# An attention and gated-MLP block on one core: reordered by a scheduler that runs at build time, part of the exponentials moved to VectorE, and full-width matmuls split into four column tiles

## The chip, the core and the metric

The kernel runs on one core of a Trainium2 chip. The metric is the time of one execution on the device in microseconds (us); lower is better. TensorE multiplies matrices, ScalarE takes exponentials, VectorE does elementwise work and copies, GpSimd does some of that too, and SyncE issues DMAs. The profile records one execution with the start, the end and the wait of every instruction, and the share of its clock that TensorE was granted (1.0 is full, 0.5 is half). "The trace" is that record, "the page" is its printed summary.

A run is called slow when it is more than 1.5% above the fastest run of the same kernel. The ratios use the fast runs; the medians are of all runs.

## The reference

One sequence of 2048 rows of 640 columns passes through a 32-head attention block (20 columns per head) and a gated MLP (1728 columns). Both have a layer norm ahead and a residual around them. All is bf16.

```python
def _A_ref(x, wqkv, wo):
    B, S, D = x.shape; H = 32; Dh = D // H          # 1, 2048, 640; Dh = 20
    q, k, v = ...(x @ wqkv) split into heads...
    scores = jnp.einsum("bhqd,bhkd->bhqk", q, k) * (Dh ** -0.5)
    p = softmax(scores, axis=-1)
    o = jnp.einsum("bhqk,bhkd->bhqd", p, v)
    return o.transpose(0, 2, 1, 3).reshape(B, S, D) @ wo
def _B_ref(x, w_gate, w_up, w_down):
    h = (x @ w_gate) * (x @ w_up)
    return h @ w_down
h  = x + _A_ref(_layernorm(x), wqkv, wo)
h2 = h + _B_ref(_layernorm(h), w_gate, w_up, w_down)
return h2
```

The scores are 32 x 2048 x 2048 exponentials. Spread over 128 partitions they make 2048 banks of 512 columns (a bank here is a PSUM tile of 128 x 512 in f32). That is the work around which both kernels are built.

## The kernel before

Attention runs in four passes of 512 queries. In a pass, each of eight groups of four heads goes through sixteen tiles of 128 keys. One step makes four score banks, takes their exponentials as two instructions of 1024 columns, and multiplies them with V ("PV") into one accumulator. All other matmuls are background: a Python generator emits some of it after each half step, a budget of 440 ns at a time. During the first pass the background is the K, Q and V projections; during every later pass it is the output projection and the MLP of the pass ahead (the one just finished).

```python
sA   = ctx.enter_context(tc.tile_pool(name="sA", bufs=3, space=PSUM))    # scores, 3 x 2 banks
accp = ctx.enter_context(tc.tile_pool(name="accp", bufs=1, space=PSUM))  # PV accumulator
mp   = ctx.enter_context(tc.tile_pool(name="mp", bufs=1, space=PSUM))    # all background: ONE bank
# ... cut ...
for c in range(KC):                       # gate, of second_stage(); up is alike
    nc.tensor.matmul(pg[0:M, :], lhsT=wg[:, c, o:o + M], rhs=ln2T[:, c, :],
                     start=(c == 0), stop=(c == KC - 1))
    yield 220
gs = p2s.tile([P, QW], F32, name="gs", tag="gs")
nc.vector.tensor_copy(gs[0:M, :], pg[0:M, :])
# ... cut ...
def emit_S(n):                            # two score banks: row tiles of the array, 32 rows each
    for i, j in enumerate(hs_):
        nc.tensor.matmul(sp[:, i, :], lhsT=kT[g][32*j:32*j+32, kt*P:(kt+1)*P],
                         rhs=qT[qc][32*j:32*j+32, g, :], start=True, stop=True)
def emit_exp(n):
    nc.scalar.activation(E[:], sp[:], ACT.Exp, scale=LN2_ / UNIT)         # 1024 columns
def emit_PV(s):                           # four column tiles, 32 columns each
    for j in range(HP):
        nc.tensor.matmul(acc[32*j:32*j+32, :], lhsT=Vx[kt][:, h*VS:h*VS+32],
                         rhs=E_of.pop((s, j)), start=(kt == 0), stop=(kt == NT - 1))
# ... cut ...
for n in range(N + LAG):
    if n + LEAD < N:
        emit_S(n + LEAD)
    if n < N:
        emit_exp(n)
    for s in pv_at.get(n, ()):
        emit_PV(s)
        # at the end of a pass: finish all background, then queue second_stage(qc)
    advance(440)
while bg:
    advance(1 << 30)                      # the last pass's output projection and MLP: the tail
```

The softmax here doesn't subtract the row's maximum and nothing guards it: scores larger than these inputs give would overflow.

Of the kernel before, what the change touches and what calls it, by code (L numbers as in the profile page):

```python
# [10 lines left out]
F32 = mybir.dt.float32  # L11
ACT = mybir.ActivationFunctionType
# [3 lines left out]
P = 128  # L16
# [9 lines left out]
NQ = S // QW  # L26
# [5 lines left out]
VW = H * VS + 32 - VS  # L32
# [3 lines left out]
EPS_B = 1.0013580322265625e-05  # L36


@with_exitstack
def kernel(  # L40
# [17 lines left out]
    dram = ctx.enter_context(tc.tile_pool(name="dram", bufs=4, space=bass.MemoryType.DRAM))  # L58


    const = ctx.enter_context(tc.tile_pool(name="const", bufs=1))
    keep = ctx.enter_context(tc.tile_pool(name="keep", bufs=1))
    xpool = ctx.enter_context(tc.tile_pool(name="xpool", bufs=1))
    epool = ctx.enter_context(tc.tile_pool(name="epool", bufs=6))
    npool = ctx.enter_context(tc.tile_pool(name="npool", bufs=2))
    tiny = ctx.enter_context(tc.tile_pool(name="tiny", bufs=2))
    lnp = ctx.enter_context(tc.tile_pool(name="lnp", bufs=1))

    sA = ctx.enter_context(tc.tile_pool(name="sA", bufs=3, space=PSUM))
    accp = ctx.enter_context(tc.tile_pool(name="accp", bufs=1, space=PSUM))  # L70
    mp = ctx.enter_context(tc.tile_pool(name="mp", bufs=1, space=PSUM))


    xt = [xpool.tile([P, TPC, D], BF16, name=f"x{c}", tag=f"x{c}") for c in range(NQ)]
    p1 = tc.alloc_tile_pool(name="p1", bufs=1, side="right")
    Wr = [p1.tile([P, 3 * D], BF16, name=f"Wr{c}", tag=f"Wr{c}") for c in range(KC)]
    for tt in range(TPC):
        nc.sync.dma_start(xt[0][:, tt, :], x2d[tt * P:(tt + 1) * P, :])
    for c in range(KC):
        eng = nc.scalar if c % 2 == 0 else nc.sync  # L80
        eng.dma_start(Wr[c][:, 0:2 * D], A_wqkv[c * P:(c + 1) * P, 0:2 * D])
    for c in range(KC):
        nc.sync.dma_start(Wr[c][:, 2 * D:3 * D], A_wqkv[c * P:(c + 1) * P, 2 * D:3 * D])
    for ch in range(1, NQ):
        nc.sync.dma_start(
            xt[ch][:], x2d[ch * QW:(ch + 1) * QW, :].rearrange("(t p) d -> p t d", p=P))

    ident = const.tile([P, P], BF16, name="ident")
    make_identity(nc, ident[:])
    half = const.tile([P, TPC], F32, name="half")  # L90
    nc.gpsimd.memset(half[:], 0.5)
    warm = const.tile([P, 1], F32, name="warm")
    nc.scalar.activation(warm[:], half[:, 0:1], ACT.Exp)

    kT = [keep.tile([P, S], BF16, name=f"kT{g}", tag=f"kT{g}") for g in range(G)]
    qT = [(p1 if ch == 0 else keep).tile([P, G, QW], BF16, name=f"qT{ch}", tag=f"qT{ch}")
          for ch in range(NQ)]
    Vx = [keep.tile([P, VW], BF16, name=f"Vx{t}", tag=f"Vx{t}") for t in range(NT)]
    OnT = [keep.tile([P, QW], BF16, name=f"On{g}", tag=f"On{g}") for g in range(G)]

    Wp = [[p1.tile([P, G * P], BF16, name=f"Wp{b}{c}", tag=f"Wp{b}{c}") for c in range(KC)]
          for b in range(2)]
    lnT = p1.tile([P, KC, S], BF16, name="lnT")
    for b in (1, 0):
        for c in range(KC):
            wv = Wp[b][c][:].rearrange("p (h e) -> p h e", e=32)
            nc.gpsimd.memset(wv[:, :, DH:32], 0.0)
    for t in range(NT):
        nc.gpsimd.memset(
            Vx[t][:, 0:H * VS].rearrange("p (h e) -> p h e", e=VS)[:, :, DH:VS], 1.0)  # L110
        nc.gpsimd.memset(Vx[t][:, H * VS:VW], 0.0)


    def ln_stats(srcs):
        mv = tiny.tile([P, TPC, 2], F32, name="mv", tag="mv")
        for i, s in enumerate(srcs):
            st = tiny.tile([P, 2, 6], F32, name="st", tag="st")
            for c in range(2):
                nc.vector.bn_stats(st[:, c, :], s[:, c * HD:(c + 1) * HD])  # L119
            nc.vector.bn_aggr(mv[:, i, :], st[:])  # L120
        vb = tiny.tile([P, TPC], BF16, name="vb", tag="vb")
        nc.vector.tensor_copy(vb[:], mv[:, :, 1])
        ve = tiny.tile([P, TPC], BF16, name="ve", tag="ve")
        nc.vector.tensor_scalar_add(ve[:], vb[:], EPS_B)
        den = tiny.tile([P, TPC], BF16, name="den", tag="den")
        nc.gpsimd.tensor_tensor(den[:], ve[:], half[:], ALU.pow)
        rstd = tiny.tile([P, TPC], F32, name="rstd", tag="rstd")
        nc.vector.reciprocal(rstd[:], den[:])
        return mv, rstd

    def ln_apply(s, i, mv, rstd):
        ln = lnp.tile([P, D], BF16, name="ln", tag=f"ln{i}")
        nc.vector.tensor_scalar(ln[:], s, mv[:, i, 0:1], rstd[:, i:i + 1],  # L133
                                ALU.subtract, ALU.mult)
        return ln

    def transposed(lns, dst, copy):

        for c0 in range(0, KC, 2):
            n = min(2, KC - c0)  # L140
            pt = mp.tile([P, 2, QW], BF16, name="pt", tag="m")
            for c in range(n):
                for i, ln in enumerate(lns):
                    nc.tensor.transpose(pt[:, c, i * P:(i + 1) * P],  # L144
                                        ln[:, (c0 + c) * P:(c0 + c + 1) * P], ident[:])
                    yield 70
            copy(dst(c0, n), pt[:, 0:n, :])


    def proj_k(g, ch, b):  # L150
        sl = slice(ch * QW, (ch + 1) * QW)
        ps = mp.tile([P, QW], F32, name="pk", tag="m")
        for c in range(KC):
            nc.tensor.matmul(ps[:], lhsT=Wp[b][c][:, g * P:(g + 1) * P], rhs=lnT[:, c, sl],  # L154
                             start=(c == 0), stop=(c == KC - 1))
            yield 220
        if b == 1:
            nc.vector.tensor_copy(kT[g][:, sl], ps[:])
        else:
            nc.vector.tensor_scalar_mul(qT[ch][:, g, :], ps[:], KAPPA)  # L160

    def proj_v(t, hf):
        ps = mp.tile([P, HD], F32, name="pv", tag="m")
        for c in range(KC):
            nc.tensor.matmul(ps[:], lhsT=lnT[:, c, t * P:(t + 1) * P],  # L165
                             rhs=Wr[c][:, 2 * D + hf * HD:2 * D + (hf + 1) * HD],
                             start=(c == 0), stop=(c == KC - 1))
            yield 140
        nh = H // 2
        nc.vector.tensor_copy(  # L170
            Vx[t][:, hf * nh * VS:(hf + 1) * nh * VS].rearrange("p (h e) -> p h e", e=VS)[:, :, 0:DH],
            ps[:].rearrange("p (h e) -> p h e", e=DH))

    done = set()

    def run(gen):
        for _ in gen:
            pass

    def lnT_dst(ch):  # L180
        return lambda c0, n: lnT[:, c0:c0 + n, ch * QW:(ch + 1) * QW]

    def ln1(ch):
        mv, rstd = ln_stats([xt[ch][:, i, :] for i in range(TPC)])
        return [ln_apply(xt[ch][:, i, :], i, mv, rstd) for i in range(TPC)]


    lns = ln1(0)
    for b in (1, 0):
        for c in range(KC):  # L190
            nc.scalar.copy(
                Wp[b][c][:].rearrange("p (h e) -> p h e", e=32)[:, :, 0:DH],
                Wr[c][:, b * D:(b + 1) * D].rearrange("p (h e) -> p h e", e=DH))
    run(transposed(lns, lnT_dst(0), nc.vector.tensor_copy))
    run(proj_k(0, 0, 1))
    run(proj_k(0, 0, 0))
    done |= {("K", 0, 0), ("Q", 0, 0)}
    ln_next = ln1(1)

    def first_stage():  # L200
        nonlocal ln_next
        for t in range(TPC):
            yield from proj_v(t, 0)
            done.add(("V", t, 0))
        for ch in range(1, NQ):
            yield from transposed(ln_next, lnT_dst(ch), nc.vector.tensor_copy)
            yield from proj_k(0, ch, 1)
            done.add(("K", 0, ch))
            if ch + 1 < NQ:
                ln_next = ln1(ch + 1)  # L210
            for t in range(ch * TPC, (ch + 1) * TPC):
                yield from proj_v(t, 0)
                done.add(("V", t, 0))
        vq = deque(range(NT))
        for g in range(1, G):
            yield from proj_k(g, 0, 0)
            done.add(("Q", g, 0))
            for ch in range(NQ):
                yield from proj_k(g, ch, 1)
                done.add(("K", g, ch))  # L220
# [79 lines left out]
    for n, (_, s, hs_) in enumerate(units):  # L300
        last_unit[s] = n
# [142 lines left out]
```

## Time and profile before

The time was 1791.87 us (median of 3 runs, 1779.78 to 1798.72).

| reading | value |
|---|---|
| TensorE, ScalarE, VectorE busy | 81%, 56%, 15% |
| exponentials | 1024 of 1024 columns, 994.5 us busy |
| first exponential; last one ends; tail after it | 23.2 us; 1627.6 us; 158 us |
| granted clock | mean 0.60 as listed, 0.56 with the head corrected (see below) |

These are lines of the page of the kernel before: busy time, the busy share and the clock in tenths over 40 slices of the span, the chain of waits that ended last, and the group of the exponentials (busy us, mean ns, then idle time ahead and what ended it).

```profile
span 1785.0 us, 15333 instructions
...
PE 1453.2 (81%) x6000; PEld 333.1 (19%) x6000; DVE 261.4 (15%) x512; ACT 1002.4 (56%) x1036; POOL 59.5 (3%) x90
...
PE   4678789889947898989958989999778898996677
...
ACT  3235445445954454699944545999544458994000
...
PEclk9999655555556555865565555755555558555557
...
PE 55%; ACT 18%; DVE 11%; issue 8%; DMA 5%; SPq 2%; POOL 1%; POOLq 0%; DVEq 0%; ACTq 0%
...
L335 ACT ACTIVATE E<-sp 128x1024 bf16<-128x1024 f32 x1024 | 994.5, 1298 | 619.1 <-PE sp L325 618.4
```

TensorE is busy and heads the chain, while ScalarE idles 619 us in wait of scores. The clock row says that TensorE ran at half clock nearly all the time. Its first slices are false. The trace's first clock record begins at 154.5 us, and the page prints 1.0 where it has none; but near 101 us the timeline shows back-to-back matmuls of 320 columns starting every 240 to 270 ns (columns of the fence: start, duration, engine, line, operation):

```profile
101.43 0.45 PE L165 MATMUL pv<-Wr_97,lnT 128*128 128x320 bf16 x1
101.67 0.47 PE L165 MATMUL pv<-Wr_98,lnT 128*128 128x320 bf16 x1
101.94 0.47 PE L165 MATMUL pv<-Wr_99,lnT 128*128 128x320 bf16 x1
```

At recorded full clock (around 750 us) matmuls of the same size start every 136 ns. So the head ran at half clock too, and in the whole span only 204 us were at full clock.

Every listed mean clock has this fault. In the traces of the experiments it is worth 0.03 or less, but in a run without a trace the head is unknown: 8 of the 29 runs of the old kernel beside the experiments list 0.70 to 0.73, and they are no faster (1766.92 to 1803.19 us). A false head that reached to the second rise of the clock in this trace, at 550.4 us, would list 0.70 (an estimate from this trace). So the listed mean of an untraced run shows little.

What a half-clock stage looks like is seen in TensorE's timeline of the kernel before, during gate and up:

```profile
640.76 0.61 PE L325 MATMUL sp<-qT_136,kT_128 32*128 32x512 bf16 x2
641.30 0.62 PE L349 MATMUL acc<-E,Vx_147 128*32 128x512 bf16 x4
641.85 1.03 PE L264 MATMUL pg<-ln2T,wg 128*128 128x512 bf16 x2
642.82 0.61 PE L325 MATMUL sp<-qT_136,kT_128 32*128 32x512 bf16 x2
```

A 512-column matmul streams for 427 ns at this clock: behind a matmul of its own shape, 96 of 122 back-to-back starts of full-width matmuls in this trace are 426 or 427 ns apart. Each change of tile shape (scores in row tiles, PV in column tiles, background at full width; "mode" in some places below) adds about 110 ns (medians of 107 to 113 ns between scores, PV and the start of background; about 100 ns at full clock): from 640.76 to 641.30 the score pair takes 540 ns and not 427. The texts below call this gap a drain; the trace shows its length and not what TensorE does in it. The old order made 1837 such changes, counted in the order of starts in the trace.

Next, windows of the kernel before (columns: window, length, busy us with count for TensorE, weight loads, VectorE, ScalarE and GpSimd, then granted clock, DMA share, GB/s): gate and up, pure attention, and the tail.

```profile
640.00:660.00 20.00, 18.20 (x61) 2.97 (x60) 2.76 (x4) 10.26 (x11) 0.00 (x0) 0.50 0.03 8
...
840.00:860.00 20.00, 18.50 (x92) 3.46 (x88) 0.00 (x0) 20.00 (x23) 1.26 (x1) 0.50 0.04 14
...
1627.00:1785.00 158.00, 102.78 (x340) 41.13 (x337) 36.51 (x68) 0.61 (x1) 2.27 (x2) 0.59 0.13 34
```

With background in the mix TensorE is full and ScalarE half used. When a pass has run out of background, ScalarE is full: an exponential of 1024 columns every 0.917 us (38 in a row from 840.8 us), of which 1024 take about 939 us.

### The profile page before, as it was taken

What the parts mean: (1) busy time and instruction counts of PE and PEld (TensorE: products, weight loads), DVE (VectorE), ACT (ScalarE), POOL (GpSimd) and SP (SyncE); (2) the same over time, 40 slices, a digit from 0 to 9 for tenths busy, and PEclk for the clock granted to TensorE, in tenths of its full rate; (3) what the DMA queues carried; (4) which work ended last, traced back from release to release, by engine and by line L of the source; (5) the groups of instructions that cost most, each with busy time, mean ns of one, the idle gap of its engine ahead of it and who ended that gap; (6) DMA issues with size and microseconds to landing.
All of it is one profiled execution on the core that took longest, in us unless ns stands there. A gap on an engine that the chain in (4) does not pass through costs nothing.

```text
span 1785.0 us, 15333 instructions
## 1 busy us (share of the span) xinstructions
PE 1453.2 (81%) x6000; PEld 333.1 (19%) x6000; DVE 261.4 (15%) x512; ACT 1002.4 (56%) x1036; POOL 59.5 (3%) x90
## 2 busy tenths in 40 slices
PE   4678789889947898989958989999778898996677
PEld 1222111111102111221121112211211122111223
DVE  4411111111002111100021111000021111000321
ACT  3235445445954454699944545999544458994000
POOL 1000000000010000000000000000000000000000
PEclk9999655555556555865565555755555558555557
DMA  3000000000013101000011010000102100001010
GB/s 114 0 1 6 7 7 0 7 7 0 9 31 78 36 15 32 18 11 13 7 36 29 22 32 10 18 7 13 36 1 51 33 2 20 13 7 42 23 48 15
DMA packets 60128, 38.33 MB, mean 21 GB/s; under 512 B 17496, under 2 KB 55320, under 8 KB 60056
## 3 DMA queue, kind: packets, MB, share of 16 engines
q1 hardware_dynamic: 59624, 36.37, 7.9%
q8 instruction: 47, 0.77, 0.2%
q10 hardware_dynamic: 432, 0.98, 0.2%
q14 instruction: 25, 0.20, 0.0%
HBM read 34.19 MB, written 2.88 MB: 21 GB/s over the span
## 4 chain that ended last, share of the span: by engine, by line
PE 55%; ACT 18%; DVE 11%; issue 8%; DMA 5%; SPq 2%; POOL 1%; POOLq 0%; DVEq 0%; ACTq 0%
ACT E L335 18%; PE sp L325 14%; PE pk L154 8%; PE pg L264 7%; PE acc L349 7%; PE pu L271 7%; PE py L284 5%; PE pv L165 2%; PE po L243 2%; DVE hh L275 2%; DMA rs<-accS 2%; SPq L359 2%; DVE gs L268 1%; DMA rb<-rd 1%; DVE st L119 1%
## 5 line engine op out<-in xcount | busy, mean ns | idle before, releaser
L335 ACT ACTIVATE E<-sp 128x1024 bf16<-128x1024 f32 x1024 | 994.5, 1298 | 619.1 <-PE sp L325 618.4
L264 PE MATMUL pg<-ln2T,wg 128*128 128x512 bf16 (+1 forms) x280 | 143.7, 617 | 59.1 <-DVE hh L275 45.5
L271 PE MATMUL pu<-ln2T,wu 128*128 128x512 bf16 (+1 forms) x280 | 144.1, 618 | 21.4 <-DVE gs L268 21.4
L284 PE MATMUL py<-Wd,hh 128*128 128x320 bf16 x448 | 98.6, 347 | 16.8 <-DVE ot L287 13.7
L356 DVE COPY accS<-acc 128x512 f32<-128x512 f32 x32 | 22.1, 692 | 405.2 <-PE acc L349 405.2
L268 DVE COPY gs<-pg 128x512 f32<-128x512 f32 (+1 forms) x56 | 38.5, 688 | 207.9 <-PE pg L264 207.9
L275 DVE TENSOR_TENSOR hh<-gs,pu 128x512 bf16<-128x512 f32 (+1 forms) x56 | 38.3, 684 | 203.5 <-PE pu L271 203.5
L144 PE MATMUL pt<-ident,ln 128*128 128x128 bf16 x160 | 25.6, 303 | 52.1 <-DVE ln L133 39.7
L284 PEld LDWEIGHTS <-hh 128*128 128x128 bf16 x448 | 41.9, 106 | 67.0 <-issue 49.9
L271 PEld LDWEIGHTS <-wu 128*128 128x128 bf16 (+1 forms) x280 | 27.4, 117 | 97.8 <-issue 97.8
L154 PE MATMUL pk<-lnT,Wp_168 128*128 128x512 bf16 x32 | 18.2, 570 | 29.1 <-DVE qT_135 L160 6.4
L264 PEld LDWEIGHTS <-wg 128*128 128x128 bf16 (+1 forms) x280 | 26.1, 120 | 83.2 <-issue 70.2
L243 PE MATMUL po<-wo,On_162 128*128 128x320 bf16 x32 | 11.6, 362 | 35.3 <-POOL On_162 L368 35.3
L243 PE MATMUL po<-wo,On_155 128*128 128x320 bf16 x32 | 11.7, 365 | 31.0 <-DMA wo<-in_A_wo_dram 26.9
L325 PEld LDWEIGHTS <-kT_128 32*128 32x128 bf16 x256 | 13.0, 98 | 125.4 <-issue 125.4
L165 PE MATMUL pv<-Wr_96,lnT 128*128 128x320 bf16 x32 | 12.6, 393 | 28.9 <-DVE Vx_147 L170 5.1
L325 PEld LDWEIGHTS <-kT_129 32*128 32x128 bf16 x256 | 13.1, 99 | 116.0 <-issue 115.8
L287 DVE TENSOR_TENSOR ot<-py,h 128x320 bf16<-128x320 f32 x32 | 15.6, 488 | 123.6 <-PE py L284 123.6
L154 PE MATMUL pk<-lnT,Wp_163 128*128 128x512 bf16 x32 | 18.6, 583 | 16.7 <-DVE qT_137 L160 5.5
L325 PEld LDWEIGHTS <-kT_131 32*128 32x128 bf16 x256 | 13.4, 99 | 86.8 <-issue 86.8
L325 PEld LDWEIGHTS <-kT_132 32*128 32x128 bf16 x256 | 13.4, 99 | 84.3 <-issue 84.3
L325 PEld LDWEIGHTS <-kT_127 32*128 32x128 bf16 x256 | 13.1, 97 | 79.6 <-issue 79.6
(225 smaller groups left out, 1592.7 us busy)
## 6 DMA issues: line engine op xcount, KB each, us to landing
rb<-rd SPq DMA_DIRECT2D x32, 256.0 KB
wg<-in_B_w_gate_dram SPq DMA_DIRECT2D x24, 320.0 KB, 6.3
wu<-in_B_w_up_dram SPq DMA_DIRECT2D x24, 320.0 KB
out_dram<-ot SPq DMA_DIRECT2D x16, 160.0 KB, 1.8
Wd<-in_B_w_down_dram SPq DMA_DIRECT2D x1, 2080.0 KB, 14.3
rs<-accS SPq DMA_DIRECT2D x128, 2.0 KB, 1.7
wg<-in_B_w_gate_dram SPq DMA_DIRECT2D x4, 240.0 KB
wu<-in_B_w_up_dram SPq DMA_DIRECT2D x4, 240.0 KB
```

The source lines that it names most:

```text
L154: nc.tensor.matmul(ps[:], lhsT=Wp[b][c][:, g * P:(g + 1) * P], rhs=lnT[:, c, sl], start=(c == 0), stop=(c == KC - 1))
L165: nc.tensor.matmul(ps[:], lhsT=lnT[:, c, t * P:(t + 1) * P], rhs=Wr[c][:, 2 * D + hf * HD:2 * D + (hf + 1) * HD], start=(c == 0), stop=(c ...
L243: nc.tensor.matmul(ps[:], lhsT=OnT[g][:, tt * P:(tt + 1) * P], rhs=wo[:, g, hsl], start=(g == 0), stop=(g == G - 1))
L264: nc.tensor.matmul(pg[0:M, :], lhsT=wg[:, c, o:o + M], rhs=ln2T[:, c, :], start=(c == 0), stop=(c == KC - 1))
L268: nc.vector.tensor_copy(gs[0:M, :], pg[0:M, :])
L271: nc.tensor.matmul(pu[0:M, :], lhsT=wu[:, c, o:o + M], rhs=ln2T[:, c, :], start=(c == 0), stop=(c == KC - 1))
L275: nc.vector.tensor_tensor(hf_t[0:M, :], gs[0:M, :], pu[0:M, :], ALU.mult)
L284: nc.tensor.matmul(ps[:], lhsT=hh[f][0:K, tt * P:(tt + 1) * P], rhs=Wd[0:K, f, hsl], start=(f == 0), stop=(f == NF - 1))
L325: nc.tensor.matmul(sp[:, i, :], lhsT=kT[g][32 * j:32 * j + 32, kt * P:(kt + 1) * P], rhs=qT[qc][32 * j:32 * j + 32, g, :], start=True, sto ...
L335: nc.scalar.activation(E[:], sp[:], ACT.Exp, scale=LN2_ / UNIT)
L349: nc.tensor.matmul(acc[32 * j:32 * j + 32, :], lhsT=Vx[kt][:, h * VS:h * VS + 32], rhs=E_of.pop((s, j)), start=(kt == 0), stop=(kt == NT - 1))
L359: nc.sync.dma_start(rs[32 * j:32 * j + 32, :], accS[32 * j + DH:32 * j + DH + 1, :])
```

## The change

The intent is to keep all three compute engines busy together. Instead of emitting in program order, the new kernel simulates the engines while it is being built, with assumed durations, and emits whatever its model says should come next. Around that:

- VectorE takes some of the 2048 score banks. It computes the exponential from the bits of a rounded integer in one pass over PSUM and four 16-bit passes over pairs of banks. ScalarE's instructions become 1536 and 1024 columns in turn, 687 of them.
- Every background matmul (transposes too) is split into four column tiles of 32 output columns, the shape of PV, so that PV and background follow each other without a change of mode.
- Background and VectorE's score banks share two PSUM banks, where background had one.
- Scores use 20 rows and not 32 per head, so the padded copies of the weights go. Most K and Q projections run at 120 dense columns, and small DMAs spread the heads.
- The fourth pass of 512 queries becomes two of 256, so that less work is left after the last exponential.

The core of the diff (about 1300 changed lines, cut):

```diff
+WIDTHS = [512, 512, 512, 256, 256]
+LAT = {"ACT": 240.0, "DVE": 230.0, "POOL": 250.0, "SP": 2300.0, "PE": 275.0}
+SWITCH = 110.0
+class Engines:                  # the model: a task has duration, dependences, priority
+    def run(self):
+        while True:             # the engine that can start earliest goes next
+            # ... cut ...
+            self.free[e] = s + t.dur
+            t.ev.t = s + t.dur + t.lat
+            t.fn()              # emits the real instruction
+class Pe:                       # picks scores, PV or background, keeping ScalarE fed
+    # ... cut ...
-    sA = ctx.enter_context(tc.tile_pool(name="sA", bufs=3, space=PSUM))
-    accp = ctx.enter_context(tc.tile_pool(name="accp", bufs=1, space=PSUM))
-    mp = ctx.enter_context(tc.tile_pool(name="mp", bufs=1, space=PSUM))
+    A3 = psum.tile([P, 3, QW], F32, name="A3", tag="A3")
+    A2 = psum.tile([P, 2, QW], F32, name="A2", tag="A2")
+    acc = psum.tile([P, QW], F32, name="acc", tag="acc")
+    mb = tiles(psum, 2, [P, QW], F32, "m")
+    def columns(ps, lhsT, rhs, start, stop, n, width=P):
+        for i in range((width + 31) // 32):
+            w = min(32, width - 32 * i)
+            mm(ps[32 * i:32 * i + w, 0:n], lhsT[:, 32 * i:32 * i + w], rhs, start, stop)
+    # VectorE's exponential: one pass per bank, then four over two banks
+    nc.vector.tensor_scalar(it[:, pos, :], bank.ap, BIAS, 0.0, ALU.add, ALU.max)
+    nc.vector.tensor_scalar(f[:, 0:n, :], it[:, 0:n, :], 127, None, ALU.bitwise_and)
+    nc.vector.tensor_scalar(h[:, 0:n, :], f[:, 0:n, :], QR, QK, ALU.subtract, ALU.mult)
+    nc.vector.tensor_tensor(fb[:, 0:n, :], h[:, 0:n, :], f[:, 0:n, :], ALU.mult)
+    nc.vector.tensor_tensor(e16[:, 0:n, :], it[:, 0:n, :], fb[:, 0:n, :], ALU.add)
-        advance(440)
+    en.run()
+D_START = 8                     # first score bank that VectorE may take
```

## The prediction

> **What bounds it now.** Span 1785 us. Page: TensorE 81% busy, ScalarE 56%, VectorE 15%. The chain of waits is 55% TensorE and 18% exp. The clock row averages 0.6 and is nearly always 0.5; its "9999" at the start is wrong: in the timeline near 101 us, 320-column matmuls follow each other every 267 ns, which is half clock. At full clock (around 750 us) they are 136 ns apart. So TensorE runs at half clock and is the limit wherever background matmuls run (time windows: 18.2 of 20 us busy, exp 10.2). Only pure attention is exp-bound: 1024 columns every 0.917 us, so 1024 of them cannot take less than 939 us.

> Summing streamed columns times array area over 3.4 us windows, every window that switched the clock up followed one with at least 0.74 of the array in use, and it fell back after 0.31 or less, never above 0.39. Gate and up stages sit at 0.73, just under.[...]

> Each change between row-tiled scores and the other matmuls costs about 110 ns (540 ns start to start for a 427 ns stream)[...].

> **What changes** (counts from the instruction order):
> - ScalarE: 1024 exps of 1024 columns become 687 of 1536 or 1024. VectorE takes 327 of 2048 score banks. ScalarE's floor: 1721 x 0.427 + 687 x 0.063 = about 780 us.
> - VectorE: 327 PSUM passes and 4 x 166 integer passes, estimated from present durations (PSUM copy 0.69 us alone, about 0.6 back to back[...]) at 520 to 600 us, plus about 240 us of evacuations and norms: 760 to 850 us. Now 261.
> - TensorE: 6000 matmuls become 12876, as quads of four columns in parallel (attention-times-V quads already start within 7 ns). About 1190 mode changes; PV to background costs none. Streams plus drains: about 680 us at full clock, about 1240 us at half clock.
> - Prologue shortens (smaller first loads); the last query pass is 256 wide, so the tail, now about 155 us, becomes about 60 us.

> **Critical path.** Three engines near 700 to 850 us, interleaved, in-order, with two PSUM banks shared by background work and VectorE scores. I expect 10 to 15% stalls. All at full clock: about 950 us with head and tail. All at half clock: about 1400 us. Background is spread over all passes and denser than before (estimate 0.76 to 0.8 of the array at half clock), so the clock should be full for most, not all, of the span. I predict **1040 us**, 80% range 930 to 1270. Chances: faster 0.97, within 2% 0.02, slower 0.01.

> **Signs.** Right: clock row mean above 0.75; ScalarE busy 75% or more; VectorE above 75%; quads 216 ns apart back to back at full clock, four members within 10 ns; tail under 70 us. Wrong: clock mostly 0.5, TensorE over 90% busy, span 1300 or more.

> **What would break it.** (1) The clock stays at half: the array-area threshold is only just passed. (2) Column-tiled weight loads are not hidden between quads, or TensorE's queue cannot issue eight instructions in 136 ns. (3) Integer passes run slower than 16-bit rate, so VectorE becomes the limit and evacuations hold the two banks. (4) The order was fixed from assumed durations; each error stalls in-order queues.

Three passages are cut where marked: two statements about the hardware, and the time of a 16-bit pass, which the trace before does not show over its range. With that time in it, VectorE's sum came to 520 to 600 us for the exponential passes and 760 to 850 us in all. The sum can't be redone from the terms that are left; no other sum, and not the 1040 us, has lost a term. (Measured after: 440 to 704 ns for a 16-bit pass over 1024 columns.)

## The result

The changed kernel took 1035.22 us (median of 4 runs, 1023.53 to 1042.09); the old one, run in the same rounds, 1785.82 us (1777.0 to 1798.72). Two of the four runs, 1039.52 and 1042.09 us, count as slow. The ratio is 0.5747, with a 95% interval of 0.5692 to 0.5801. A ratio here is the mean time of one kernel's fast runs over that of the other's in the same rounds, so it is not quite the ratio of the medians. The result was correct against the reference, as were those of all experiments below.

These are the lines of the page after that answer to those above:

```profile
span 1021.8 us, 29998 instructions
...
PE 829.9 (81%) x12876; PEld 341.9 (33%) x12876; DVE 790.7 (77%) x1549; ACT 794.1 (78%) x695; POOL 62.8 (6%) x62
...
PE   4788887868726798889987888889879888978867
...
DVE  6679776689726999989879989998797998366243
ACT  3569777798745999999998999999898997087400
...
PEclk9899977799756989999979999999887999978989
...
PE 30%; DVE 24%; ACT 17%; DMA 10%; issue 9%; SPq 8%; POOL 1%; DVEq 0%; POOLq 0%; ACTq 0%
...
L457 ACT ACTIVATE E<-A 128x1536 bf16<-128x1536 f32 (+1 forms) x687 | 788.9, 1287 | 148.7 <-PE A L318 68.4
...
L470 DVE TENSOR_SCALAR i<-m 128x512 int16<-128x512 f32 x331 | 226.3, 684 | 37.6 <-PE m L318 36.2
...
L506 DVE TENSOR_TENSOR fr<-hl,fr 128x1024 bf16<-128x1024 bf16 (+1 forms) x166 | 116.1, 700 | 2.5
L509 DVE TENSOR_TENSOR ED<-i,fr 128x1024 int16<-128x1024 int16 (+1 forms) x166 | 116.9, 704 | 1.5
...
L503 DVE TENSOR_SCALAR hl<-fr 128x1024 bf16<-128x1024 int16 (+1 forms) x166 | 74.5, 449 | 4.2
L500 DVE TENSOR_SCALAR fr<-i 128x1024 int16<-128x1024 int16 (+1 forms) x166 | 73.1, 440 | 2.8
```

Three engines now share the span at 77 to 81%, and the chain is spread over all of them. TensorE executes more than twice the matmuls, most of them a quarter of an old one that run four at a time, in 623 us less busy time. Its streams would take about 640 us before and 570 us after if all ran at full clock (an estimate from columns and overlaps in the traces), so most of the fall is the clock, which is at full for 801 us. (Clock records begin at 19.0 us here, so this row can be trusted.) VectorE's five passes sum to 607 us. Over 1024 columns the passes with one input (L500, L503) take 440 and 449 ns in the mean and those with two (L506, L509) 700 and 704 ns, 251 to 264 ns more. The int16 passes go at the rate of the bf16 ones: by the medians of the trace 426 ns with an int16 output against 427 with a bf16 one for one input, 681 against 682 ns for two.

Windows of the kernel after: one of the steady state, the two around its first hole, its second hole, and the tail.

```profile
380.00:400.00 20.00, 16.79 (x214) 5.43 (x211) 19.37 (x35) 20.00 (x19) 1.27 (x1) 1.00 0.24 57
...
280.00:300.00 20.00, 7.01 (x52) 1.75 (x52) 6.12 (x11) 11.52 (x11) 4.37 (x1) 0.63 0.45 77
300.00:320.00 20.00, 5.40 (x42) 1.27 (x41) 7.32 (x12) 4.44 (x4) 1.55 (x1) 0.50 0.51 148
...
864.00:892.00 28.00, 26.21 (x642) 17.39 (x639) 12.51 (x27) 0.21 (x1) 1.41 (x2) 1.00 0.20 52
...
959.00:1022.00 63.00, 45.95 (x1164) 31.43 (x1161) 22.83 (x56) 0.20 (x1) 2.15 (x3) 0.92 0.39 87
```

In the stage where the old kernel had ScalarE 10.3 us busy of 20, the new one has it busy without a gap, with gate and up running beside it. TensorE's timeline after, in that stage, reads:

```profile
401.91 0.39 PE L318 MATMUL A<-qT,kT 20*128 20x512 bf16 x3
402.23 0.61 PE L318 MATMUL m<-ln2T,wg 128*32 128x512 bf16 x8
```

Eight column-tile matmuls are two quads. Successive quads start 216 ns apart, the four members of one within about 10 ns (median of the trace; nine in ten within 22 ns). Quads of 320 columns start 136 ns apart. Their 128-row weight loads, four to a quad and 97 to 102 ns each in the mean, add nothing that shows: in the trace before, full-width matmuls of 512 columns with one load each start 215 to 227 ns apart at full clock (9 pairs).

Two holes remain, each about 23 to 28 us of an idle ScalarE. The first is at 287 to 314 us. In the timeline after (SPq is SyncE's queue of DMA issues; a bracket gives the idle time before the instruction and what ended it):

```profile
287.23 4.37 POOL L870 MEMSET wo<- 128x5120 bf16 x1 [16.24 <-DMA qT<-stg]
...
291.62 1.51 SPq L871 DMA_DIRECT2D wo<-in_A_wo_dram  x4
...
295.50 5.04 SPq L939 DMA_DIRECT2D wu<-in_B_w_up_dram  x1
...
303.00 2.48 SPq L585 DMA_DIRECT2D rs<-accS  x4
...
310.83 0.25 DVE L587 RECIPROCAL rr<-rs 128x16 f32<-128x16 f32 x1 [23.85 <-DMA rs<-accS]
...
315.05 1.02 ACT L457 ACTIVATE E<-A 128x1024 bf16<-128x1024 f32 x1 [23.07 <-PE m L318]
```

The softmax sums of a finished head group travel by a 2 KB DMA to be inverted. Its issue stands in SyncE's queue behind the weights of the second stage, and those wait for the first stage: `wo` is issued at 291.62 us, after its memset, which took 4.37 us and had waited 16.24 us for a transfer of the first stage (`qT`). That the second stage takes over the memory of the first is read from the kernel. VectorE's reciprocal waits 23.85 us for the sums. VectorE starts nothing else in that time: the pass L500 on banks that were read by 286.98 us starts at 311.00, behind the reciprocal. PV waits in turn (22.88 us, for the result of L509), and ScalarE (23.07 us). The second hole, at 864 us:

```profile
869.04 17.20 PE L318 MATMUL m<-Wd,hh 128*32 128x320 bf16 x448
...
886.17 4.53 PE L318 MATMUL m<-wo,On 128*32 128x320 bf16 x128
...
889.84 1.41 POOL L599 TENSOR_TENSOR On<-accS,rb 128x256 bf16<-128x256 f32 x2 [57.91 <-PE m L318]
...
892.49 3.71 ACT L457 ACTIVATE E<-A 128x1536 bf16<-128x1536 f32 x3 [28.29 <-PE acc L318]
```

Here TensorE executes 576 background matmuls in a row. The normalised output `On` of the current pass may not be written before the output projection of the pass ahead has read it, and that projection stands behind the down projection.

### The profile page after: what moved, and what is told of

Same layout as the page of the kernel before. It is cut to its first block, busy times and chain, and to the rows that moved or that the text cites. A ratio compares the mean times of both kernels' runs of the same rounds, so it can differ in the third digit from the quotient of the medians.

```text
span 1021.8 us, 29998 instructions
## 1 busy us (share of the span) xinstructions
PE 829.9 (81%) x12876; PEld 341.9 (33%) x12876; DVE 790.7 (77%) x1549; ACT 794.1 (78%) x695; POOL 62.8 (6%) x62
## 4 chain that ended last, share of the span: by engine, by line
PE 30%; DVE 24%; ACT 17%; DMA 10%; issue 9%; SPq 8%; POOL 1%; DVEq 0%; POOLq 0%; ACTq 0%
ACT E L457 17%; PE m L318 16%; PE A L318 7%; PE acc L318 6%; DVE i L470 6%; DMA rs<-accS 5%; SPq L585 4%; DVE fr L506 3%; DVE ED L509 3%; SPq L811 2%; DVE hl L503 2%; DVE fr L500 2%; DMA wg<-in_B_w_gate_dram 1%; DVE gs L946 1%; DVE hh L956 1%
## 5 line engine op out<-in xcount | busy, mean ns | idle before, releaser
L457 ACT ACTIVATE E<-A 128x1536 bf16<-128x1536 f32 (+1 forms) x687 | 788.9, 1287 | 148.7 <-PE A L318 68.4
L318 PE MATMUL A<-qT,kT 20*128 20x512 bf16 (+1 forms) x2150 | 288.4, 363 | 83.4 <-ACT E L457 75.6
L470 DVE TENSOR_SCALAR i<-m 128x512 int16<-128x512 f32 x331 | 226.3, 684 | 37.6 <-PE m L318 36.2
L318 PE MATMUL acc<-E,Vx 128*32 128x512 bf16 (+1 forms) x2150 | 194.6, 376 | 2.5 <-DVE accS L582 1.3
L318 PE MATMUL acc<-ED,Vx 128*32 128x512 bf16 (+1 forms) x410 | 122.4, 378 | 37.4 <-DVE ED L509 37.0
L318 PE MATMUL m<-qT,kT 20*128 20x512 bf16 (+1 forms) x410 | 136.5, 365 | 4.8 <-DVE i L470 4.7
L506 DVE TENSOR_TENSOR fr<-hl,fr 128x1024 bf16<-128x1024 bf16 (+1 forms) x166 | 116.1, 700 | 2.5
L509 DVE TENSOR_TENSOR ED<-i,fr 128x1024 int16<-128x1024 int16 (+1 forms) x166 | 116.9, 704 | 1.5
L318 PE MATMUL m<-ln2T,wg 128*32 128x512 bf16 (+1 forms) x1350 | 96.3, 370 | 12.1 <-DMA wg<-in_B_w_gate_dram 5.0
L318 PE MATMUL m<-ln2T,wu 128*32 128x512 bf16 (+1 forms) x1350 | 92.3, 357 | 8.9 <-DVE gs L946 4.3
L503 DVE TENSOR_SCALAR hl<-fr 128x1024 bf16<-128x1024 int16 (+1 forms) x166 | 74.5, 449 | 4.2
L500 DVE TENSOR_SCALAR fr<-i 128x1024 int16<-128x1024 int16 (+1 forms) x166 | 73.1, 440 | 2.8
```

The lines of the kernel that those rows point to most:

```text
L318: nc.tensor.matmul(out_, lhsT=lhsT, rhs=rhs, start=start, stop=stop)
L457: nc.scalar.activation(E[:, 0:size, :], src[:, 0:size, :], ACT.Exp, scale=LN2_ / UNIT)
L470: nc.vector.tensor_scalar(it[:, pos, :], bank.ap, BIAS, 0.0, ALU.add, ALU.max)
L500: nc.vector.tensor_scalar(f[:, 0:n, :], it[:, 0:n, :], 127, None, ALU.bitwise_and)
L503: nc.vector.tensor_scalar(h[:, 0:n, :], f[:, 0:n, :], QR, QK, ALU.subtract, ALU.mult)
L506: nc.vector.tensor_tensor(fb[:, 0:n, :], h[:, 0:n, :], f[:, 0:n, :], ALU.mult)
```

## The experiments

Each kernel differs from the old or the new one by the edit shown. Experiments e1 to e4 ran on one chip, e5 to e8 on another, e9 to e11 on a third; each had runs of the old kernel beside it, with medians of 1784 to 1790 us. The theory going in was that the gain is a product of three parts: background in column tiles puts the array's use over the 0.74 or more that the rises of the old trace had followed, VectorE relieves ScalarE once TensorE is no longer the limit, and the scheduler overlaps them.

### e1: no score banks for VectorE

```diff
-D_START = 8
+D_START = 1 << 30
```

> The changed kernel with no score bank on VectorE (the scheduler lays out the rest anew). My theory: the gain is mostly TensorE at full clock under a full interleave, and VectorE's share of the exps is a minor part of it. Then the exps alone need 410 x 1.343 + 409 x 0.917 = 926 us (from the counts and the present durations) and the run takes 1080 to 1150 us, ScalarE above 85% busy, VectorE below 35%, mean clock 0.85 or more. Rival A: taking the exps off ScalarE is the main gain; then 1300 us or more.

Measured: 1133.78 us (median, 1127.73 to 1139.95), ratio 0.6333 (0.6285 to 0.6381). ScalarE is busy 950.0 us (84%), VectorE 22%, mean clock 0.773. So VectorE's share of the exponentials is worth about 100 us of the 750 (1134 less 1034; 93 to 105 us by the ratios, as e5 ran on another chip). The time came as the theory expected it; the clock did not. It fell to 0.77, where I had expected it to stay at 0.85 or more. Why is not shown: TensorE's score matmuls did not wait longer for ScalarE (65.8 us in 139 waits, against 75.6 us in 177 in the changed kernel).

### e2: background at full width in the new kernel

```diff
-        for i in range((width + 31) // 32):
-            w = min(32, width - 32 * i)
-            mm(ps[32 * i:32 * i + w, 0:n], lhsT[:, 32 * i:32 * i + w], rhs, start, stop)
+        mm(ps[0:width, 0:n], lhsT[:, 0:width], rhs, start, stop)
```

(The transposes likewise.)

> The changed kernel in the same order, with every background matmul and transpose but the two gathered head projections as one full-width 128-column matmul in place of a quad. My theory: what column tiling saves is only the drains between attention-times-V and background, 223 of them x 0.107 us = 24 us at most, and the clock holds: 1035 to 1075 us, mean clock 0.85 or more. Rival B: the column tiling is what keeps the clock up; then mean clock 0.75 or less and 1150 us or more. Rival C: quads cost issue time and full width is faster than 1020 us.

Measured: 1050.59 us (1048.45 to 1070.55), ratio 0.5862 (0.5807 to 0.5918), mean clock 0.859. In the new order the column tiling is worth only about 17 us by the times of the fast runs (1051.7 less the 1034.6 of e5, on another chip; 9 to 20 us by the ratios, whose intervals overlap with those of e5 and of the result). The saved changes of shape alone could account for it: 223 changes between PV and background x 0.107 us is 24 us. But the clock was lower too (0.859, 0.905 in e5), and this run does not tell the two apart.

### e3: the old kernel with its background in column tiles, nothing else

```diff
+    def cols(out_, lhsT, rhs, start, stop):
+        width = lhsT.shape[-1]
+        for i in range((width + 31) // 32):
+            w = min(32, width - 32 * i)
+            nc.tensor.matmul(out_[32 * i:32 * i + w, :], lhsT=lhsT[:, 32 * i:32 * i + w], rhs=rhs,
+                             start=start, stop=stop)
-                nc.tensor.matmul(pg[0:M, :], lhsT=wg[:, c, o:o + M], rhs=ln2T[:, c, :],
+                cols(pg[0:M, :], lhsT=wg[:, c, o:o + M], rhs=ln2T[:, c, :],
```

(All background matmuls and transposes alike.)

> The kernel before, with only its background matmuls and transposes column-tiled. My theory of the clock (about 0.74 to 0.77 of the array must be in use over a 3.4 us window to switch it up): gate and up stages stood at 0.73; one of five drains per cycle goes away, which gives about 0.75 to 0.76, so many of those windows trip: mean clock 0.68 or more (it was 0.60 by the page, with the false start) and 1450 to 1680 us. Rival: the clock does not react to density, only one drain in five is saved: 1700 to 1790 us, clock as before.

Measured: 1529.23, 1559.54, 1569.17 and 1570.0 us, median 1564.36, against 1790.11 for the old kernel beside it. The three longer runs count as slow by the rule. The listed clock goes with the times (0.76 in the shortest run, 0.72 in the profiled one), but the head of the untraced run is unknown. I use the median, about 226 us saved; the one fast run alone would give 261. The same column tiling that was worth about 17 us in the new order is worth 226 us in the old one. The changes of shape that it saves there are 273 x 0.107 = 29 us (an estimate from the trace's count of changes from PV to background). The rest goes with the clock: 634 us at full clock in place of 204.

That the clock rose is shown; that it rose because a threshold of area was passed is not. Of the 25 rises in this trace 15 followed windows of 0.717 to 0.744, under the 0.75 to 0.76 that I had expected, and every half-clock window above 0.728 was followed by a rise, while in the old trace 17 windows of 0.74 to 0.76 were not. So with column tiling the clock rose at lower area sums than before, and what it reacts to is not settled.

A window of this experiment at full clock, in a gate and up stage like that of 640 us above:

```profile
580.00:600.00 20.00, 17.03 (x211) 5.44 (x211) 3.92 (x6) 15.89 (x16) 0.00 (x0) 1.00 0.01 2
```

### e4: the old kernel, the first matmul of each background sum done twice

This one tells "the clock" from "fewer changes of shape". It only adds work (272 matmuls, whose results are overwritten; the trace recorded 217 of them), and its trace has the same 1837 changes of tile shape as the old kernel's, but it fills the array a little more.

```diff
+    def twice(out_, lhsT, rhs, start, stop):
+        if start:
+            nc.tensor.matmul(out_, lhsT=lhsT, rhs=rhs, start=True, stop=True)
+        nc.tensor.matmul(out_, lhsT=lhsT, rhs=rhs, start=start, stop=stop)
```

> The kernel before, with the first matmul of every background sum issued twice (272 matmuls more, the same result). If time only follows work, this costs about 272 x 0.4 = 105 us: 1850 to 1900 us. My theory: the extra matmul raises the array's use in the gate and up stages from 0.73 to about 0.75 and the clock switches up in many of them, so the run gets no slower and perhaps faster, 1550 to 1780 us, with the mean clock 0.65 or more, although it does more.

Measured: 1620.94, 1658.16, 1679.74 and 1695.19 us, median 1668.95: with more work the kernel is about 121 us shorter. (The three longer runs count as slow by the rule; the fast one alone would give 169 us. All four are faster than every run of the old kernel.) The rival, by which added matmuls can only cost time, fell. TensorE's timeline of this run shows the moment. In the area sums the window from 592.8 us has 0.77 of the array, and at 596.2 us the clock record turns to 1.0:

```profile
594.10 0.61 PE L330 MATMUL sp<-qT,kT 32*128 32x512 bf16 x2
594.63 0.62 PE L354 MATMUL acc<-E,Vx 128*32 128x512 bf16 x4
595.19 0.61 PE L116 MATMUL pu<-ln2T,wu 128*128 128x512 bf16 x1
595.59 0.89 PE L117 MATMUL pu<-ln2T,wu 128*128 128x512 bf16 x2
596.41 0.39 PE L330 MATMUL sp<-qT,kT 32*128 32x512 bf16 x2
596.73 0.60 PE L117 MATMUL pu<-ln2T,wu 128*128 128x512 bf16 x2
```

The score pair takes 0.39 us where it took 0.61, and with 0.4 to 0.6 of the array in use the clock then stays up to 620 us at least (1.00 in the mean of 600 to 620 us). In all, 607 us ran at full clock, against 204 in the old kernel.

### e5: the changed kernel again

No edit; it is the base for the three that ran beside it.

> The changed kernel again, unaltered, so that the next three are compared with it in the same rounds on the same chip. 1020 to 1045 us.

Measured: 1033.86 us (1028.31 to 1043.35), ratio 0.5812 (0.5777 to 0.5847).

### e6: the second stage's weight loads made to wait for the softmax sums

This tests the first hole: if the queue order is its cause, issuing the weights after the last normalisation of the first pass must close it.

```diff
-        e0 = en.add("POOL", 4400.0, [], lambda: nc.gpsimd.memset(p2["wo"][:], 0.0), 2)
+        late = on_ev[0, G - 1]
+        e0 = en.add("POOL", 4400.0, [late], lambda: nc.gpsimd.memset(p2["wo"][:], 0.0), 2)
# w_down in 14 loads of one row block each, and x, w_gate, w_up: each gets `late` as a dependence
```

> The changed kernel with the second stage's weight loads held back until the first pass's last softmax normalisation is through, and the 2 MB w_down load cut into 14. My theory of the hole at 287 to 314 us (VectorE waits 23.9 us in order for a 2 KB load that stands behind w_gate, w_up and w_down on the one queue, and TensorE and ScalarE wait for VectorE): the hole goes, 1000 to 1018 us, no stretch of 20 us with ScalarE under 8 us busy before the last 100 us apart from the one near 870 us. Rival: the hole has another cause (the half clock, or the memory hand-over of the weight tiles), the time stays within 1025 to 1045 us and the hole stays.

Measured: 1018.41 us (1013.1 to 1022.24), ratio 0.5719 (0.569 to 0.5747); fast mean 1018.0 against 1034.6 for e5. The gap is gone: ScalarE is busy 17.59 us of the window 280 to 300 (11.52 before the edit) and 11.72 of 300 to 320 (4.44). Closing a hole of 23 us was worth 16.6 us.

### e7: e6, and the two narrow passes write different halves of `On`

This tests the second hole: the last pass no longer has to wait for the output projection of the pass ahead.

```diff
-            deps.append(wo_done.get(p - 1))
+            deps.append(wo_done.get(p - 2 if p == 4 else p - 1))
+        o0 = w if p == 4 else 0
-            OnT[g][:, 0:w], a[:, 0:w], b[:, 0:w], ALU.mult), 1)
+            OnT[g][:, o0:o0 + w], a[:, 0:w], b[:, 0:w], ALU.mult), 1)
# the last output projection reads the same half; cut, as is the edit of e6
```

> As the run before, and the last 256-wide pass writes its attention output into the unused half of the tiles, so that its normalisation no longer waits for the output projection of the pass ahead. In the changed kernel ScalarE stands idle for 28 us near 865 to 892 us while TensorE does 688 background matmuls in one go. My theory: the idle time there is real for ScalarE but TensorE is busy in it, and the same matmuls move into the tail (1860 in place of 1182 after the last score), so this gains little: 0 to 10 us against the late loads alone. Rival: ScalarE's 28 us are on the critical path and come off in full, 20 to 28 us.

Measured: 1013.16 us, fast mean 1014.6, ratio 0.5699 (0.5667 to 0.5732), so 3.4 us less than e6, and not clear of noise (the intervals overlap). The gap of 28 us on ScalarE is gone and the last exponential ends 31 us sooner (915.6 for 946.7 us), but the tail grows from 64.6 to 97.2 us. In the hole TensorE was doing background that had to be done at some time; without the hole it is done in the tail. Idle time of ScalarE cost little or nothing there.

### e8: four passes of 512 in the new kernel

```diff
-WIDTHS = [512, 512, 512, 256, 256]
+WIDTHS = [512, 512, 512, 512]
```

> The changed kernel with four query passes of 512 in place of 512, 512, 512, 256, 256. My theory: the narrow last passes only shorten the tail (63 us after the last exp in the changed kernel, 158 us before): the tail grows to 90 to 115 us, and the total by 20 to 45 us against the changed kernel in the same rounds, less what the stall near 870 us gives back. Rival: no difference within 1%.

Measured: fast runs 1004.72, 1014.22 and 1014.67 us, slow ones 1023.55 to 1025.0; median of all 1019.11, ratio 0.5671 (0.5619 to 0.5722). My expectation was wrong. The tail did grow as expected, to 85.7 us from 63, but the total fell by 15 us (medians) to 23 us (fast means). The last exponential ends at 927.1 us in place of 959.2: the second hole is absent, and there are 11312 matmuls in place of 12876, because two passes of 256 load every weight twice. The narrow passes cost more than the shorter tail gave. How much of that is the hole and how much the extra weight loads is not told apart.

### e9: e6 and e8 together

```diff
-WIDTHS = [512, 512, 512, 256, 256]
+WIDTHS = [512, 512, 512, 512]
# and the edit of e6
```

> The two edits that helped, put together: late weight loads (16 us in the same rounds) and four 512-wide passes (15 to 23 us). If they remove different waits, the hole of 23 us near 296 us that the four-pass run still shows goes too: 990 to 1005 us. If they overlap, 1008 to 1020 us. The tail stays at about 86 us.

Measured: 990.34 us (988.46 to 997.25, six runs, all fast), ratio 0.5548 (0.5523 to 0.5572). The two edits add up, as expected, and this is the fastest version. Its timeline at the place of the first hole:

```profile
294.97 2.45 SPq L585 DMA_DIRECT2D rs<-accS  x4
298.70 0.25 DVE L587 RECIPROCAL rr<-rs 128x16 f32<-128x16 f32 x1 [2.63 <-DMA rs<-accS]
...
307.75 2.17 SPq L880 DMA_DIRECT2D Wd<-in_B_w_down_dram  x2
```

The sums now go ahead of the weights, and the reciprocal waits 2.63 us in place of 23.85. ScalarE has no gap over 6.1 us from its first to its last exponential.

### e10: e3, with the background paced over the whole pass

Could the old kernel, once column-tiled, be had cheaply to the new one's speed by spreading its background? The edit is e3's, and:

```diff
-        advance(440)
+        advance(440 if n < per_qc else 240)
```

> The kernel before with column-tiled background (1529 to 1570 us) and, from the second query pass on, background paced at 240 in place of 440 per exp, so that it spreads over the whole pass in place of its first two thirds. Simple view: spreading evens the load, exps run at about 18 of 20 us all through and each later pass falls from about 325 to 285 us: 1400 to 1460 us. My theory of the clock: spread thinner, the array's use at half clock falls to about 0.67, below the 0.74 that switches the clock up, so the clock stays at half, TensorE becomes the limit in all of the pass and nothing is won: 1530 to 1680 us, mean clock 0.62 or less.

Measured: 1625.31 us (1622.19 to 1628.35), ratio 0.9095 (0.9056 to 0.9134): 55 to 96 us slower than e3's runs (on another chip). The simple view (spreading balances TensorE and ScalarE, 1400 to 1460 us) fell. The time was in the range of the clock theory, but its mechanism missed: the clock did not stay at half. Its mean was 0.718 as listed (0.69 with the head corrected), where I had expected 0.62 or less; it rose 25 times, as in e3, and was at full for 610 us against e3's 634. In windows of 40 us it swung between 0.5 and 0.96. What the loss comes from is therefore not settled: the background still ended before the pass did, and a stretch of pure attention remained.

### e11: the new kernel with neither VectorE's exponentials nor the column tiling

e1 and e2 together:

```diff
-D_START = 8
+D_START = 1 << 30
-        for i in range((width + 31) // 32):
-            w = min(32, width - 32 * i)
-            mm(ps[32 * i:32 * i + w, 0:n], lhsT[:, 32 * i:32 * i + w], rhs, start, stop)
+        mm(ps[0:width, 0:n], lhsT[:, 0:width], rhs, start, stop)
```

This leaves the scheduler, the wider exponentials and the PSUM arrangement.

> The changed kernel without VectorE's score banks (1134 us, clock 0.77) and with full-width background in that order. In the changed kernel full width cost 16 us and 0.04 of clock. Without VectorE's banks a burst has 2 or 3 scores in place of up to 4, the array is used less, and the clock should be nearer its threshold. If so, losing the quads costs more here: 1160 to 1230 us, mean clock 0.70 or less. Rival: the same 10 to 25 us, 1145 to 1158 us, clock 0.73 or more.

Measured: 1160.47 us (1159.11 to 1161.48), ratio 0.6493 (0.6466 to 0.6521), mean clock 0.758 (0.773 in e1), 1596 changes of mode in the trace. Column tiling is worth 27 us here. My expectation, that without VectorE's banks the clock would hang on the column tiling as it does in the old order, was not supported: the time was at the lower edge of the range, and the clock was as high as the rival had it.

### The parts side by side

| version | median us |
|---|---|
| old (beside the experiments) | 1784 to 1790 |
| old + column tiling (e3) | 1564 |
| new order, no VectorE exponentials, no column tiling (e11) | 1160 |
| + column tiling (e1) | 1134 |
| + VectorE exponentials = the change (e5) | 1034 |
| + late weight loads and four passes (e9) | 990 |

The rows come from three chips. The parts do not add. Column tiling is worth 226 us in the old order and 17 to 27 us in the new one. The likely reason is that both the tiling and the new order get the old clock problem out of the way, and it can be removed only once: at full clock were 204 us in the old kernel, 634 in e3, and already 579 in e11, without the tiling.

## Why the prediction was right, and where it was not

The total, 1040 us, was 0.5% from the 1035.22 measured, and the reasons behind it held in the main. That it came so close is in part luck: the stated range was 930 to 1270 us, the share of the span at full clock was a guess between 950 and 1400 us, VectorE's terms cancelled, and the narrow passes cost time that the prediction counted as gained. Point by point:

- **"TensorE runs at half clock and is the limit"**: right. e4 shows it best: more work at a higher clock was 121 us faster. The threshold "at least 0.74 of the array" led to the right forecast that the clock would rise in e3 and e4, though in e3 most rises came at or under it. In the changed kernel it is not sharp either: clocks rose after windows of 0.63 to 0.98, stayed down at up to 0.73, and fell after 0.37 or less. So the threshold describes the old trace, and the rule behind it is not settled.
- **Clock "full for most, not all, of the span", above 0.75**: right, 0.90, with 801 us at full clock. The reason given, 0.76 to 0.8 of the array at half clock, fits only on the median: the windows before a rise had 0.77 there, between 0.63 and 0.98.
- **TensorE "about 680 us at full clock", "about 1190 mode changes"**: right. The trace has 1188 changes, and about 570 us of streams with 0.1 us for each change make about 690 us (an estimate from the trace).
- **ScalarE floor of 780 us and 75% busy**: right, exponentials 788.9 us, ScalarE 78%.
- **VectorE 760 to 850 us**: right in sum, 790.7 us, with terms that missed and cancelled. The exponential passes took 607 us (predicted 520 to 600), all else about 184 us (predicted 240). Giving VectorE this work was worth 100 us (e1).
- **"PV to background costs none"**: right (at full clock and 512 columns background starts 216 ns after the last matmul of PV, median of 39, where two quads of one kind are 206 ns apart so counted and a change of shape adds about 100), but the share that column tiling has of the gain was not in the prediction. In the new order it is about 17 us (e2), in the old one 226 us (e3).
- **"10 to 15% stalls"**: about right. ScalarE stood idle for 149 us, 16% of the 937 us from its first to its last exponential. The first hole was an in-order wait, worth 16.6 us (e6). The second, of 28 us, cost only 3.4 us, within the noise (e7).
- **"Prologue shortens"**: wrong. The first exponential starts at 22.1 us, after 23.2. The head was 1 us shorter, no more.
- **"The tail becomes about 60 us"**: right, 63 us. But taking it as a gain was wrong: the narrow passes that make the tail short cost more than they save (e8), so the change would have been 15 to 23 us faster without them.
- **Quads "216 ns apart", "four members within 10 ns"**: both right, by the medians of the trace. The feared limit on issue did not show: eight instructions (four loads, four matmuls) per 136 ns were sustained. PV quads of the old kernel start within 10 ns too (all 510 found whole in its trace), where the prediction has 7.

What stays open is the largest part. From 1786 to 1160 us (e11) the gain of 626 us comes with the new order, the wider exponentials, the second background bank and the other rearrangements together. The traces show where the old kernel lost it (half clock in gate and up, 158 us of tail, a gap of 27 us at the end of the first pass), and e11 had 579 us at full clock and a tail of 60 us. The wider exponentials alone could save little: all columns take about 939 us in the old form and about 926 in the new one (an estimate, 2048 banks x 0.427 us + 819 instructions x 0.063 us; in the trace after, back-to-back instructions of 1536 and 1024 columns start 1.346 and 0.918 us apart in the mean). But no run here tells the scheduler apart from the second bank.

## What to carry to other kernels

Read the spacing of back-to-back matmuls before believing a busy share: an 81% busy TensorE streamed at half the speed that it reached elsewhere in the same trace, and a small change in the work, even useless matmuls, brought full clock for 607 of 1678 us (e4). The worth of one edit depends on which others are in: test it in both the old and the new surroundings before ranking it. When one queue carries both bulk loads and small latency-critical transfers, put the small ones ahead (16.6 us in e6); and close a hole only after asking what the other engines were doing in it (28 us closed for 3.4 us in e7).
